# Attention by clusters ahead of two gated layers: products of the identity between TensorE's first steps, centroid norms as steps of the plan, the second pair's loads issued later, and a new table of places

## The chip, the cores and the metric

The kernel runs on one core of one Trainium2 chip. The metric is the device time of one launch in microseconds; the time before is the median of three runs, 766.34 us (765.43 to 766.65). The profile is one execution recorded on the chip. TensorE appears as PE (matmuls) and PEld (weight loads), VectorE as DVE, ScalarE as ACT, GpSimd as POOL, SyncE as SP; SPq and ACTq are the queues from which SyncE and ScalarE issue DMAs.

## What is computed

```python
q_n = q / (norm(q) + 1e-6);  k_n = ...;  c_n = centroids / (norm(centroids) + 1e-6)
q_assign = argmax(einsum('bhsd,hcd->bhsc', q_n, c_n), -1)      # 2 x 8 heads, 768 tokens, D 64, 16 centroids
k_assign = argmax(einsum('bhsd,hcd->bhsc', k_n, c_n), -1)
scores = where(q_assign == k_assign, q @ k.T / 8, -1e9)
attn = exp(scores - max);  attn = attn / (sum(attn) + 1e-9);  x = attn @ v      # (1536, 512)
h = relu(x @ w_in);   x = (h * h) @ w_out                        # d_ff 2048
h = x @ w2_in;        out = (h * cos(h)) @ w2_out
```

## The kernel before

Two heads are worked on together, so there are eight pairs; a pair has 768 queries and 768 keys. For each pair the kernel goes through the same steps, each a small function that issues a few instructions:

- **Preparation.** `load_raw` brings q and k (384 KB each, transposed) into `fq` and `fk`. `sims` multiplies them with the centroid directions `cb` on TensorE (L415); `keep_sims` scales the result by the inverse centroid norms `cn` on ScalarE (L425, tile `sc`); `by_token` transposes it on TensorE (L433); `largest` takes the maximum over the 16 centroids on VectorE (L440, `mx`); `spread` copies it out on ScalarE (L447, `mxb`); `at_max` transposes it back (L456); `compare` (L463), `one_hot` (TensorE, L469) and `keep_one_hot` (VectorE, L476, `ot`) make the one-hot rows of the assignment. `high_part` and `low_part` split q and k into a rounded part and its rest (tiles `set`). `stage`, `stage_oh` and `stage_own` move such rows by DMA into the tiles `ext` (called `xq`, `xk` in the code) and `set`, from which TensorE reads them.
- **Maxima.** `s_max` multiplies one block of queries with half of the keys (L500, four products into a double bank `unit`), `s_largest` takes the row maxima on VectorE (L510); a pair has twelve such steps. After the six of one half, `max_parts` (L519), `max_cast`, `max_rows` (TensorE, L534), `max_keep` and `stage_max` (DMA `set<-mr`) bring the maxima to where the scores need them.
- **Scores.** `scores` (L567, eight products; the last two read the staged maxima), `exponent` on ScalarE (L577), `add_up` on GpSimd (L589, two additions a step), `pv` on TensorE (L597), then `sums` (L612, reads GpSimd's additions) and the steps of the division.

The order of all this is written out: `PLACES` gives each call of each step a number, the steps are sorted by it, and every engine gets its instructions in that order. An engine never overtakes in its own queue. What stands ahead of the sorted steps (L693 to L737) is issued first on each engine: the loads of the first pair, the centroids, their squares, sums, power and inverse (L702 to L704, L734, L735), the zeroing of `ext` on GpSimd (L686), 26 small products of the identity on TensorE (`warm`, L681), and a table for choosing the first of equal maxima (L711 to L726). The second pair's `load_raw` has the places 0 and 11, ahead of nearly everything else, and the first pair's v the place 12.

`small` hands out the one bank (`o_ps[1]`) that all steps of preparation and `sums` share; `unit` hands out one of three double banks. From about 232 us on TensorE works through the two layers (L773, L826), whose order is not in the table.

Of the kernel before, what the change touches and what calls it, by code (L numbers as in the profile page):

```python
# [28 lines left out]
WARM = 26  # L29
N_SPLIT = 54  # L30
# [6 lines left out]
        4, 5, 7, 20, 69, 100, 181, 187, 258, 257, 413, 442, 523, 566, 684, 683,  # L37
    ),
    "low_part": (
        6, 25, 44, 57, 95, 101, 186, 209, 321, 274, 414, 449, 540, 573, 776, 718,  # L40
    ),
# [3 lines left out]
    "sims": (  # L45
        1, 18, 54, 163, 299, 441, 563, 694,
    ),
    "keep_sims": (
        2, 19, 55, 169, 308, 443, 564, 696,
    ),  # L50
    "by_token": (
        3, 28, 67, 216, 349, 477, 610, 726,
    ),
    "largest": (
        8, 29, 68, 217, 350, 479, 612, 728,
    ),
    "spread": (
        9, 30, 77, 230, 356, 497, 624, 737,
    ),
    "at_max": (  # L60
        10, 31, 78, 231, 380, 498, 633, 742,
    ),
    "compare": (
        17, 35, 83, 236, 381, 509, 653, 769,
    ),
    "one_hot": (
        21, 37, 89, 288, 416, 541, 670, 794,
    ),
    "keep_one_hot": (
        23, 41, 140, 293, 423, 552, 671, 810,  # L70
    ),
    "stage_own": (
        32, 93, 282, 327, 332, 652, 611, 751,
    ),
    "stage": (
        16, 14, 60, 42, 200, 160, 277, 279, 415, 405, 587, 570, 719, 677, 799, 798,
    ),
    "stage_oh": (
        24, 72, 159, 307, 433, 589, 698, 839,
    ),  # L80
    "max_parts": (
        58, 80, 143, 184, 244, 302, 403, 447, 504, 593, 635, 713, 788, 848, 883, 962,
    ),
    "max_cast": (
        64, 85, 148, 185, 270, 303, 404, 471, 532, 597, 660, 714, 795, 849, 892, 963,
    ),
    "max_rows": (
        65, 90, 166, 219, 289, 352, 420, 478, 543, 613, 675, 741, 796, 851, 894, 971,
    ),
    "max_keep": (  # L90
        66, 91, 170, 223, 290, 353, 422, 486, 544, 614, 676, 743, 807, 852, 896, 972,
    ),
    "stage_max": (
        73, 127, 171, 238, 304, 354, 431, 488, 558, 636, 691, 762, 811, 871, 929, 984,
    ),
    "cast_selection": (
        13,
    ),
    "constants_own": (
        117, 22, 92,  # L100
    ),
    "constants": (
        48, 63,
    ),
    "move_out": (
        151, 232, 284, 337, 383, 464, 539, 596, 667, 739, 804, 853, 913, 943, 989,
    ),
    "sums": (
        152, 205, 265, 335, 406, 467, 525, 599, 658, 715, 790, 867, 910, 957, 1015,
    ),  # L110
    "move_sums": (
        153, 206, 271, 336, 407, 470, 526, 602, 659, 716, 792, 877, 930, 973, 1016,
    ),
    "deal_sums": (
        182, 218, 305, 338, 417, 502, 583, 603, 672, 738, 800, 891, 933, 992, 1018,
    ),
    "invert": (
        191, 250, 306, 360, 419, 505, 584, 649, 674, 748, 817, 897, 945, 993, 1025,
    ),
    "store_inverse": (  # L120
        240, 269, 339, 361, 455, 524, 590, 650, 717, 754, 845, 907, 949, 994,
    ),
    "load_inverse": (
        259, 276, 340, 372, 456, 536, 631, 682, 732, 775, 846, 908, 966, 995,
    ),
    "divide": (
        260, 325, 398, 399, 483, 537, 645, 704, 733, 834, 861, 934, 999, 1017,
    ),
    "combine_high": (
        261, 363, 418, 424, 550, 595, 697, 711, 744, 835, 880, 935, 1028, 1019,  # L130
    ),
    "combine_low": (
        272, 364, 454, 484, 574, 623, 708, 785, 780, 881, 914, 960, 1029, 1020,
    ),
    "s_max": (
# [5 lines left out]
    ),  # L141
    "s_largest": (
# [5 lines left out]
    ),  # L148
    "scores": (
# [5 lines left out]
    ),  # L155
    "exponent": (
# [35 lines left out]
def tile_kernel(ctx: ExitStack, tc: tile.TileContext, q, k, v, directions, centroids, w1i, w1o, w2i, w2o, out):  # L192
# [137 lines left out]
    def small():  # L330
        return free_small.pop(0)

    def give_small(u):
        free_small.append(u)
# [73 lines left out]

    def sims(n):
        d = pd[n]  # L410
        u = small()
        for i, x in enumerate("qk"):
            for h in range(2):
                g = GC * (2 * i + h)
# [705 lines left out]
```

## Time and profile before

| what | us |
|---|---|
| median of three runs | 766.34 |
| the profiled execution | 766.31 |
| its span | 764.5 |
| TensorE busy | 743.0 (97%) |
| VectorE busy | 584.0 (76%) |
| GpSimd busy | 252.1 (33%) |

The span is what the trace shows from the first to the last instruction; 1.8 us of the profiled execution lie outside it. The busy shares are means over stages with different limits: GpSimd works for most of the first 250 us and hardly afterwards. A line of the timeline gives the start, the duration, the engine, the line of the kernel, the tile written and read, how many instructions were merged, and in brackets the idle time before it with what ended it.

### The profile page before, as it was taken

To read this page: it belongs to the slowest core of one execution; us is meant where nothing else is said; L and a number is where in the kernel's file an instruction comes from. 1 tells how busy PE (TensorE), PEld (TensorE's weight loads), DVE (VectorE), ACT (ScalarE), POOL (GpSimd) and SP (SyncE) were. 2 spreads that over 40 slices of the span, in tenths; PEclk is the share of its full clock that TensorE was granted. 3 is DMA by queue.
4 is the path that set the end of the run, shared out by engine and by line. 5 is a ranking of instruction groups with operands and counts; after the bars stand their busy time and mean duration, and the time that the engine had idled before them with its cause. 6 is when DMAs were issued, how large, how long until landed. Compare 5 with 4: busy or idle time off the path is not lost.

```text
span 764.5 us, 11142 instructions
## 1 busy us (share of the span) xinstructions
PE 743.0 (97%) x4162; PEld 573.7 (75%) x4162; DVE 584.0 (76%) x915; ACT 348.8 (46%) x597; POOL 252.1 (33%) x254
## 2 busy tenths in 40 slices
PE   5899999999999999999999999999999999999998
PEld 2567666667566788888888888888887888888886
DVE  2878879878899999978874119689999766666665
ACT  2256465575464465454445325443434433343332
POOL 6598889999999420000000000012222000000000
PEclk9999999999999999999999999999999999999999
DMA  5531445243345430075300007530000100010001
GB/s 161 173 100 36 132 112 176 79 121 109 118 152 190 153 139 33 29 247 166 111 0 1 1 29 222 190 110 1 0 1 2 55 1 1 0 56 1 0 1 55
DMA packets 43113, 62.35 MB, mean 82 GB/s; under 512 B 8496, under 2 KB 31284, under 8 KB 43060
## 3 DMA queue, kind: packets, MB, share of 16 engines
q1 hardware_dynamic: 42660, 61.03, 25.3%
q10 hardware_dynamic: 400, 0.62, 0.3%
q8 instruction: 32, 0.52, 0.3%
q14 instruction: 21, 0.17, 0.1%
HBM read 48.43 MB, written 5.29 MB: 70 GB/s over the span
## 4 chain that ended last, share of the span: by engine, by line
PE 75%; issue 11%; DMA 5%; POOL 4%; DVE 2%; SPq 1%; ACT 1%; POOLq 0%; ACTq 0%; DVEq 0%
PE bank L826 28%; PE o_ps L773 13%; PE bank L773 13%; PE unit L567 8%; PE o_ps L597 6%; PE unit L500 4%; POOL ewr L811 3%; DMA set<-mr 2%; POOL acc L589 1%; DVE m L510 1%; DMA fk<-in_k_dram 1%; PE o_ps L612 1%; PE o_ps L415 1%; DMA row<-dealt 1%; DMA rb<-row 1%
## 5 line engine op out<-in xcount | busy, mean ns | idle before, releaser
L589 POOL TENSOR_TENSOR acc<-acc,p 128x384 f32<-128x384 f32 x128 | 140.0, 1126 | 0.3 <-ACT p L577 0.3
L826 PE MATMUL bank<-w,ewr 128*128 128x512 f32 x576 | 138.7, 390 | 0.4 <-POOL ewr L811 0.4
L826 PE MATMUL bank<-ewr,w 128*128 128x512 f32 x576 | 138.5, 389 | 0.0
L811 POOL TENSOR_TENSOR ewr<-ews,ewr 128x512 fp32r<-128x512 f32 x24 | 32.4, 1350 | 304.1 <-ACT ewr L807 290.1
L773 PE MATMUL bank<-xh,w 128*128 128x512 f32 x392 | 128.7, 390 | 0.0
L826 PEld LDWEIGHTS bank<-w,ewr 128*128 128x128 f32 x576 | 107.7, 188 | 24.1 <-ACT ewr L807 1.1
L826 PEld LDWEIGHTS bank<-ewr,w 128*128 128x128 f32 x576 | 108.1, 188 | 22.7 <-ACT ews L788 0.3
L773 PE MATMUL o_ps<-xh,w 128*128 128x512 f32 x376 | 123.3, 389 | 0.0
L510 DVE TENSOR_REDUCE m<-unit 128x2 f32<-128x768 f32 x96 | 88.1, 949 | 21.4 <-PE unit L500 18.8
L577 ACT ACTIVATE p<-unit 128x768 f32<-128x768 f32 x96 | 72.2, 815 | 50.5 <-PE unit L567 50.2
L811 DVE TENSOR_TENSOR ewr<-ews,ewr 128x512 fp32r<-128x512 f32 x72 | 49.5, 688 | 55.4 <-ACT ewr L790 50.7
L773 PEld LDWEIGHTS bank<-xh,w 128*128 128x128 f32 x392 | 73.6, 188 | 16.1 <-issue 0.9
L773 PEld LDWEIGHTS o_ps<-xh,w 128*128 128x128 f32 x376 | 70.6, 188 | 14.6
L798 ACT ACTIVATE ews<-ews,narrow_t 128x512 f32<-128x512 f32 x48 | 34.8, 726 | 100.3 <-DVE ews L797 100.3
L773 PE MATMUL bank<-xl,w 128*128 128x512 f32 x196 | 76.3, 389 | 0.0
L773 PE MATMUL o_ps<-xl,w 128*128 128x512 f32 x188 | 73.1, 389 | 0.0
L567 PE MATMUL unit<-set,set 64*128 64x384 f32 x512 | 69.0, 342 | 1.3 <-DMA set<-mr 1.1
L597 PE MATMUL o_ps<-p,rawv 128*64 128x384 f32 x384 | 67.9, 493 | 1.0 <-DMA rawv<-in_v_dram 1.0
L567 PEld LDWEIGHTS unit<-set,set 64*128 64x128 f32 x512 | 48.4, 184 | 9.2 <-DMA set<-mr 3.0
L298 DVE SCALAR_TENSOR_TENSOR top<-wraw,top 128x512 uint32<-128x512 uint32 x64 | 52.1, 815 | 1.6
L296 DVE SCALAR_TENSOR_TENSOR aux<-wraw,aux 128x512 f32<-128x512 uint32 x64 | 52.1, 814 | 1.5
L792 DVE TENSOR_SCALAR ews<-ews 128x512 f32<-128x512 f32 x48 | 20.3, 422 | 42.3 <-ACT ews L802 42.2
(117 smaller groups left out, 1046.1 us busy)
## 6 DMA issues: line engine op xcount, KB each, us to landing
wraw<-in_moe_w_in_dram SPq DMA_DIRECT2D x32, 512.0 KB, 4.5
wraw<-in_moe_w_out_dram SPq DMA_DIRECT2D x32, 512.0 KB, 3.5
rawv<-in_v_dram SPq DMA_DIRECT2D x8, 384.0 KB, 5.3
ext<-set SPq DMA_DIRECT2D x32, 96.0 KB, 2.3
rb<-row SPq DMA_DIRECT2D x32, 96.0 KB, 2.7
fq<-in_q_dram SPq DMA_DIRECT2D x7, 384.0 KB, 5.1
fk<-in_k_dram SPq DMA_DIRECT2D x7, 384.0 KB
held<-kept SPq DMA_DIRECT2D x8, 256.0 KB, 3.2
```

The source lines that it names most:

```text
L296: cost(690, lambda: ve.scalar_tensor_tensor(restf, low, 2.0**-32, rest, ALU.mult, ALU.add)),
L298: cost(690, lambda: ve.scalar_tensor_tensor(top, high, 0xC0000000, top, ALU.bitwise_and, ALU.bitwise_or)),
L500: nc.tensor.matmul(u[:, j, :HALF], lhsT=a[r, qs], rhs=b[r, ks], start=(p == 0), stop=(p == 1))
L510: nc.vector.tensor_reduce(d["m"][:, i, :, kh], u[:, :, :HALF], AX, ALU.max)
L567: nc.tensor.matmul(u[:, j, :HALF], lhsT=a[r], rhs=b[r, qs], start=(p == 0), stop=(p == len(ops) - 1))
L577: nc.scalar.activation(t, u[:, :, :HALF], AF.Exp, scale=SCALE)
L589: nc.gpsimd.tensor_tensor(accs[hb][:, j], a[:, j], ptiles[u_][:, j], ALU.add)
L597: nc.tensor.matmul(o_ps[0][j * D : (j + 1) * D, :HALF], lhsT=raw[n, "v"][:, kt, j, :], rhs=t[:, j], start=(kt == 0), stop=(kt == NT - 1),)
L773: nc.tensor.matmul(ph, lhsT=w[:, a, :], rhs=x[blk][:, a, :], start=(a == i == 0), stop=(a == KD - 1 and i == 2))
L798: nc.scalar.activation(e2, e2, AF.Sin, bias=hpi)
L811: e.tensor_tensor(al, e2, ah.bitcast(F32), ALU.subtract)
L826: nc.tensor.matmul(y, lhsT=a, rhs=b, start=(idx in opens and i == 0), stop=(idx in closes and i == 2))
```

## The change

`keep_warm`, a product of the identity with three copies of itself (384 columns, into `o_ps[0]`), is added and called 38 times, at places from 4 to 108. The centroid norms become steps: `squares`, `norms` and `inverses`, once for the first pair's column and once for the other three, with the centroids loaded in two pieces (32 KB by ScalarE's queue, 96 KB by SyncE's). The zeroing of `ext` for the first pair goes from GpSimd to VectorE and the first pair's rounded q from VectorE to ScalarE. The second pair's preparation takes its bank from `unit` in place of `small`. All other steps are the same instructions at other places.

```diff
 PLACES = {
...
     "load_raw": (
-        12, 0, 11, 129, 27, 26, 278, 45, 94, 370, 110, 128, 568, 392, 344, 727, 472, 556, 847, 555, 664, 915,
+        112, 13, 37, 177, 74, 82, 385, 176, 165, 402, 335, 280, 496, 436, 288, 771, 555, 618, 886, 590, 557,
+        935,
     ),
...
-    def small():
-        return free_small.pop(0)
+    def small(n=0):
+        return unit() if n == 1 else free_small.pop(0)
...
+    def keep_warm():
+        nc.tensor.matmul(
+            o_ps[0][:, :HALF].rearrange("p (a c) -> p a c", c=P), lhsT=identr,
+            rhs=identr.unsqueeze(1).to_broadcast([P, HT, P]), start=True, stop=True,
+        )
...
-    nc.scalar.dma_start(cw, centroids)
+    nc.scalar.dma_start(cw[:, :1], centroids[:, :1])
     load_raw(0, "k", (nc.sync, nc.scalar))
+    nc.sync.dma_start(cw[:, 1:], centroids[:, 1:])
     nc.scalar.activation(eps, half_t, AF.Exp)
-    constants(nc.gpsimd, xq[0])
-    nc.vector.tensor_tensor(cw, cw, cw, ALU.mult)
-    nc.vector.tensor_reduce(cn, cw, AX, ALU.add)
-    nc.gpsimd.tensor_tensor(cn, cn, half_t.to_broadcast([P, NP]), ALU.pow)
     nc.gpsimd.memset(eps, 1e-9)
+    which = slice(0, 1), slice(1, NP)
+
+    def squares(i):
+        w = which[i]
+        nc.vector.tensor_tensor(cw[:, w], cw[:, w], cw[:, w], ALU.mult)
+        nc.vector.tensor_reduce(cn[:, w], cw[:, w], AX, ALU.add)
+
+    def norms(i):
+        w = which[i]
+        nc.gpsimd.tensor_tensor(cn[:, w], cn[:, w], half_t.to_broadcast([P, w.stop - w.start]), ALU.pow)
+
+    def inverses(i):
+        w = which[i]
+        nc.vector.tensor_scalar(cn[:, w], cn[:, w], 1e-6, None, ALU.add)
+        nc.vector.reciprocal(cn[:, w], cn[:, w])
...
     warm(WARM)
-    nc.vector.tensor_scalar(cn, cn, 1e-6, None, ALU.add)
-    nc.vector.reciprocal(cn, cn)
-    constants(nc.gpsimd, xk[0])
+    constants(nc.vector, xq[0])
+    constants(nc.vector, xk[0])
...
-            at(high_part, n, x, *(() if n else (nc.vector,)))
+            at(high_part, n, x, *((nc.vector,) if n == 0 and x == "k" else ()))
...
+    for i in range(2):
+        for f in (squares, norms, inverses):
+            at(f, i)
     at(cast_selection)
+    for i in range(N_WARM):
+        at(keep_warm)
```

The lines of the changed kernel stand 15 to 37 lower than before: sims L430, by_token L448, at_max L471, one_hot L484, s_max L515, scores L582, `keep_warm` L699.

On TensorE the first pair's preparation is followed, before, by the second pair's, in the one bank `o_ps_66` (these are the rows behind the 26 small products):

```order
L415 MATMUL o_ps_66<-fq_123,cb 32x384 x2
L415 MATMUL o_ps_66<-fk_128,cb 32x384 x2
L433 MATMUL o_ps_66<-ident,sc_192 128x128 x3
L456 MATMUL o_ps_66<-ident,mxb_203 128x128 x3
L415 MATMUL o_ps_66<-fq_186,cb 32x384 x2
L415 MATMUL o_ps_66<-fk_208,cb 32x384 x2
L469 LDWEIGHTS first_of
L469 MATMUL o_ps_66<-eq_220,first_of 128x384
L433 MATMUL o_ps_66<-ident,sc_226 128x128 x3
L456 MATMUL o_ps_66<-ident,mxb_252 128x128 x3
L500 MATMUL unit_70<-set_1_106,set_0_105 128x384 x2
```

The same place now (`fq_123` and `fk_128` are the first pair, `fq_208` and `fk_241` the second):

```order
L699 MATMUL o_ps_65<-identr 128x384 x2
L430 MATMUL o_ps_66<-fq_123,cb 32x384 x2
L430 MATMUL o_ps_66<-fk_128,cb 32x384 x2
L699 MATMUL o_ps_65<-identr 128x384 x10
L448 MATMUL o_ps_66<-ident,sc_210 128x128 x3
L699 MATMUL o_ps_65<-identr 128x384 x7
L471 MATMUL o_ps_66<-ident,mxb_229 128x128 x3
L699 MATMUL o_ps_65<-identr 128x384 x3
L484 LDWEIGHTS first_of
L484 MATMUL o_ps_66<-eq_243,first_of 128x384
L699 MATMUL o_ps_65<-identr 128x384 x5
L430 MATMUL unit_70<-fq_208,cb 32x384 x2
```

Ten, seven, three and five products stand ahead of the four steps that follow, and the second pair's similarities come behind the first pair's one-hot; its at_max comes five s_max later than before.

On SyncE's queue, before, the second pair's loads (`fq_186`, `fk_208`) and v stand right behind the first pair's k:

```order
L380 DMA fq_123<-in_q_dram 64x768
L697 DMA cb<-in_directions_dram 128x128
L380 DMA fk_128<-in_k_dram 64x768
L380 DMA fq_186<-in_q_dram 128x768
L380 DMA fk_208<-in_k_dram 128x768
L375 DMA rawv_210<-in_v_dram 128x768
L405 DMA ext_1_118<-set_1_106 32x768 x2
L270 DMA wraw_0_0_216<-in_moe_w_in_dram 128x4x256
```

The same place now (`ext_1_118` is staged from the rounded k of the first pair, `set_1_106`):

```order
L395 DMA fq_123<-in_q_dram 64x768
L718 DMA cb<-in_directions_dram 128x128
L395 DMA fk_128<-in_k_dram 64x768
L721 DMA cw<-in_centroids_dram 128x192
L285 DMA wraw_0_0_200<-in_moe_w_in_dram 128x4x256
L420 DMA ext_1_118<-set_1_106 32x768 x2
L395 DMA fq_208<-in_q_dram 128x768
L395 DMA fk_241<-in_k_dram 128x768
```

A weight block of 512 KB is now what is issued right behind the first pair's k; the second pair's loads stand behind the staging of `set_1_106`, and v has gone further back.

On VectorE, now, the first rows are these (the centroids' first column is `128x64`, `narrow_t` holds the norms, `set_1_106` is the first pair's rounded k):

```order
L707 MEMSET ext_0_117 32x768 x2
L707 MEMSET ext_1_118 32x768 x2
L728 TENSOR_TENSOR cw<-cw 128x64
L729 TENSOR_REDUCE narrow_t<-cw 128x1
L712 MEMSET set_0_113 32x256 x2
L712 MEMSET set_1_114 32x256 x2
L712 MEMSET set_2_115 32x256 x2
L404 CAST set_1_106<-fk_128 128x768
L737 TENSOR_SCALAR narrow_t<-narrow_t 128x1
L738 RECIPROCAL narrow_t<-narrow_t 128x1
L455 TENSOR_REDUCE mx_225<-o_ps_66 128x24
```

Before, the inverse norms stood ahead of both roundings of the first pair, and no memset stood here.

## Rows read from the trace of the kernel before

**Rows 1.** Busy time of each engine in three stretches.

```profile
0.00:33.00 33.00, 20.84 (x123) 11.09 (x123) 16.59 (x27) 7.87 (x15) 21.85 (x45) 1.00 0.54 161
33.00:250.00 217.00, 211.92 (x1795) 141.68 (x1797) 184.81 (x229) 122.80 (x218) 198.21 (x186) 1.00 0.42 125
250.00:760.00 510.00, 509.61 (x2246) 420.75 (x2247) 381.46 (x659) 217.75 (x364) 32.02 (x25) 1.00 0.17 57
```

**Rows 2.** Whom TensorE waited for from 0 to 33 us: total, times, longest.

```profile
PE o_ps L415 <- DMA fk<-in_k_dram: 2.7, 1, 2.7
```

**Rows 3.** Whom TensorE waited for from 33 to 250 us.

```profile
PE o_ps L612 <- POOL acc L589: 1.7, 2, 0.9
```

**Rows 4.** Timeline of TensorE: the small products, first and later steps.

```profile
1.71 2.95 PE L681 MATMUL o_ps<-identb 128*128 128x128 bf16 x26 [1.71 <-DVE identb L226]
9.21 1.50 PE L415 MATMUL o_ps<-fk,cb 128*32 128x384 f32 x4 [2.65 <-DMA fk<-in_k_dram]
11.47 0.87 PE L433 MATMUL o_ps<-ident,sc 128*128 128x128 f32 x3 [0.77 <-ACT sc L425]
...
22.89 0.52 PE L500 MATMUL unit<-ext,ext 64*128 64x384 f32 x2
...
24.81 0.35 PE L500 MATMUL unit<-set,set 64*128 64x384 f32 x2
...
30.54 0.52 PE L433 MATMUL o_ps<-ident,sc 128*128 128x128 f32 x3
...
32.91 0.62 PE L567 MATMUL unit<-set,set 64*128 64x384 f32 x4
```

**Rows 5.** Timeline of VectorE: squares, rounding of k, first reduction, maxima.

```profile
7.02 0.43 DVE L702 TENSOR_TENSOR cw<-cw 128x256 f32<-128x256 f32 x1 [5.24 <-DMA cw<-in_centroids_dram]
...
10.30 1.17 DVE L389 CAST set<-fk 128x768 fp32r<-128x768 f32 x1
...
22.84 1.82 DVE L510 TENSOR_REDUCE m<-unit 128x2 f32<-128x768 f32 x2 [0.34 <-PE unit L500]
...
29.49 0.15 DVE L519 TENSOR_REDUCE m<-m 128x6 f32<-128x12 f32 x1
```

**Rows 6.** Timeline of ScalarE, of SyncE's queue and of GpSimd.

```profile
10.75 0.58 ACT L425 ACTIVATE sc<-o_ps,narrow_t 128x384 f32<-128x384 f32 x1 [6.35 <-PE o_ps L415]
...
11.50 1.22 SPq L405 DMA_DIRECT2D ext<-set  x2
...
38.88 1.98 POOL L589 TENSOR_TENSOR acc<-p,p 128x384 f32<-128x384 f32 x2
```

**Rows 7.** Stretches as in rows 1; the last number is GB/s moved.

```profile
0.00:5.00 5.00, 2.95 (x26) 2.69 (x26) 0.36 (x2) 1.49 (x2) 2.45 (x12) 1.00 0.59 158
5.00:10.00 5.00, 2.29 (x8) 0.40 (x8) 1.69 (x5) 0.00 (x0) 1.85 (x3) 1.00 0.80 268
```

**Rows 8.** The chain that ended last: start us, us, what.

```profile
2.33 6.83 DMA fk<-in_k_dram
```

**Rows 9.** DMA issues of the page: KB each, median us to landing.

```profile
ext<-set SPq DMA_DIRECT2D x32, 96.0 KB, 2.3
...
fq<-in_q_dram SPq DMA_DIRECT2D x7, 384.0 KB, 5.1
```

**Rows 10.** Groups on VectorE and ScalarE from 0 to 24 us, busy, mean ns.

```profile
L440 DVE TENSOR_REDUCE mx<-o_ps 128x24 f32<-128x384 f32 x2 | 1.1, 557 | 2.0 <-PE o_ps L433 2.0
L447 ACT COPY mxb<-mx 128x384 f32<-128x384 f32 x2 | 1.0, 511 | 3.2 <-DVE mx L440 3.2
L463 DVE TENSOR_TENSOR eq<-sc,o_ps 128x384 bf16<-128x384 f32 x2 | 1.1, 554 | 3.1 <-PE o_ps L456 3.1
L476 DVE TENSOR_SCALAR ot<-o_ps,oh_above,oh_scale 128x384 fp32r<-128x384 f32 x1 | 0.7, 677 | 2.9 <-PE o_ps L469 2.9
```

**Rows 11.** Groups of GpSimd and VectorE from 33 to 250 us.

```profile
L589 POOL TENSOR_TENSOR acc<-acc,p 128x384 f32<-128x384 f32 x128 | 140.0, 1126 | 0.3 <-ACT p L577 0.3
...
L691 DVE MEMSET set<- 32x256 f32 x6 | 1.6, 272 | 0.4
```

More of the change, by code (lines that the diff above doesn't have):

```diff
@@ L29 @@
 WARM = 26
+N_WARM = 38
 N_SPLIT = 54
@@ L44 @@
+        935,
     ),
     "sims": (
-        1, 18, 54, 163, 299, 441, 563, 694,
+        6, 52, 98, 215, 359, 469, 632, 730,
     ),
     "keep_sims": (
-        2, 19, 55, 169, 308, 443, 564, 696,
+        14, 58, 99, 217, 368, 472, 643, 731,
     ),
     "by_token": (
-        3, 28, 67, 216, 349, 477, 610, 726,
+        25, 63, 109, 265, 397, 529, 651, 772,
     ),
     "largest": (
-        8, 29, 68, 217, 350, 479, 612, 728,
+        26, 64, 114, 281, 398, 538, 656, 777,
     ),
     "spread": (
-        9, 30, 77, 230, 356, 497, 624, 737,
+        28, 72, 120, 282, 414, 551, 657, 779,
@@ L59 @@
     ),
     "at_max": (
-        10, 31, 78, 231, 380, 498, 633, 742,
+        36, 91, 121, 287, 415, 552, 665, 787,
     ),
     "compare": (
-        17, 35, 83, 236, 381, 509, 653, 769,
+        38, 97, 122, 291, 422, 564, 673, 788,
     ),
     "one_hot": (
-        21, 37, 89, 288, 416, 541, 670, 794,
+        42, 111, 147, 330, 458, 587, 703, 831,
     ),
     "keep_one_hot": (
-        23, 41, 140, 293, 423, 552, 671, 810,
+        45, 117, 148, 341, 460, 588, 717, 836,
     ),
     "stage_own": (
-        32, 93, 282, 327, 332, 652, 611, 751,
+        75, 170, 235, 283, 515, 568, 821, 944,
@@ L74 @@
     ),
     "stage": (
-        16, 14, 60, 42, 200, 160, 277, 279, 415, 405, 587, 570, 719, 677, 799, 798,
+        46, 10, 125, 104, 242, 220, 369, 353, 452, 446, 589, 576, 757, 687, 856, 863,
     ),
     "stage_oh": (
-        24, 72, 159, 307, 433, 589, 698, 839,
+        53, 143, 207, 362, 461, 601, 759, 864,
     ),
     "max_parts": (
-        58, 80, 143, 184, 244, 302, 403, 447, 504, 593, 635, 713, 788, 848, 883, 962,
+        95, 138, 196, 257, 318, 381, 439, 502, 580, 611, 688, 762, 817, 888, 949, 999,
@@ L92 @@
     ),
     "stage_max": (
-        73, 127, 171, 238, 304, 354, 431, 488, 558, 636, 691, 762, 811, 871, 929, 984,
+        123, 164, 231, 275, 354, 424, 468, 521, 594, 637, 708, 780, 851, 909, 981, 1030,
+    ),
+    "squares": (
+        0, 27,
+    ),
+    "norms": (
+        2, 56,
+    ),
+    "inverses": (
+        12, 57,
     ),
     "cast_selection": (
-        13,
+        7,
+    ),
+    "keep_warm": (
+        4, 5, 15, 16, 17, 18, 19, 20, 21, 22, 23, 24, 29, 30, 31, 32, 33, 34, 35, 39, 40, 41, 47, 48, 49, 50,
+        51, 59, 60, 61, 62, 76, 77, 85, 86, 90, 92, 108,
@@ L98 @@
     ),
     "constants_own": (
-        117, 22, 92,
+        1, 69, 81,
     ),
     "constants": (
-        48, 63,
+        100, 101,
     ),
     "move_out": (
-        151, 232, 284, 337, 383, 464, 539, 596, 667, 739, 804, 853, 913, 943, 989,
+        213, 232, 336, 358, 466, 546, 593, 666, 727, 805, 877, 921, 969, 1012, 1049,
     ),
     "sums": (
-        152, 205, 265, 335, 406, 467, 525, 599, 658, 715, 790, 867, 910, 957, 1015,
+        200, 254, 320, 386, 453, 517, 572, 645, 693, 764, 824, 885, 938, 1010, 1062,
@@ L119 @@
     ),
     "store_inverse": (
-        240, 269, 339, 361, 455, 524, 590, 650, 717, 754, 845, 907, 949, 994,
+        266, 311, 361, 435, 544, 603, 672, 719, 758, 807, 873, 942, 997, 1042,
     ),
     "load_inverse": (
-        259, 276, 340, 372, 456, 536, 631, 682, 732, 775, 846, 908, 966, 995,
+        312, 374, 445, 444, 563, 629, 677, 736, 786, 822, 893, 952, 1026, 1050,
     ),
     "divide": (
-        260, 325, 398, 399, 483, 537, 645, 704, 733, 834, 861, 934, 999, 1017,
+        342, 396, 470, 478, 583, 682, 713, 752, 815, 846, 933, 1000, 1054, 1055,
@@ L328, in tile_kernel, with give_small @@
     free_small = [o_ps[1].rearrange("p (a c) -> p a c", a=1)]
[L330 to L334 removed]
+    def small(n=0):
+        return unit() if n == 1 else free_small.pop(0)
+    def give_small(u, n=0):
+        (free_units if n == 1 else free_small).append(u)
     def unit():
@@ L410, in sims @@
         d = pd[n]
-        u = small()
+        u = small(n)
         for i, x in enumerate("qk"):
@@ L425, in keep_sims @@
         nc.scalar.activation(sc, u[:, 0, :HALF], AF.Copy, scale=cn[:, pairs[n][1] : pairs[n][1] + 1])
-        give_small(u)
+        give_small(u, n)
     def by_token(n):
         d = pd[n]
-        u = small()
+        u = small(n)
         for t in range(HT):
@@ L440, in largest @@
         nc.vector.tensor_reduce(mx, u[:, 0, :HALF].rearrange("p (g c) -> p g c", c=NC), AX, ALU.max)
-        give_small(u)
+        give_small(u, n)
     def spread(n):
@@ L452, in at_max @@
         d = pd[n]
-        u = small()
+        u = small(n)
         for t in range(HT):
@@ L463, in compare @@
         nc.vector.tensor_tensor(eq, d["sc"], u[:, 0, :HALF], ALU.is_equal)
-        give_small(u)
+        give_small(u, n)
     def one_hot(n):
         d = pd[n]
-        u = small()
+        u = small(n)
         nc.tensor.matmul(u[:, 0, :HALF], lhsT=first_of, rhs=d["eq"], start=True, stop=True)
```

24 lines of the change are left out of this document (12 added, 12 removed), and 66 rows, old and new, of the table PLACES.

## The prediction

> **What bounds the kernel now.** I read the busy time by stretches first. The reader is to see that TensorE works for 211.9 of the 217 us from 33 to 250 us, and for 509.6 of 510 us after that, but only for 20.8 of the first 33 us [rows 1]. So the end moves with the moment at which TensorE becomes full, less whatever work was done before that moment, and the change's edits all lie ahead of it. GpSimd is close behind: 198.2 of 217 us. Then I read whom TensorE waits for. Before 33 us the longest single wait is for the first pair's k, 2.7 us [rows 2]; from 33 to 250 us all its idle time is 217 - 211.9 = 5.1 us, of which 1.7 us are waits of the sums for GpSimd's additions [rows 3]. The timeline shows a second loss in the first stretch: the same three transposes take 0.87 us at 11.47 and 0.52 us at 30.54, and a pair of 384-column products takes 0.52 us at 22.89 and 0.35 us at 24.81 [rows 4]. Until about 24 us TensorE therefore works at its slower pace, although the column of the granted clock says 1.00 throughout [rows 1]; it has stood idle for 12.2 of the first 33 us. It gets faster only after a stretch without gaps. Last I followed the order of the first pair: k lands at 2.33 + 6.83 = 9.16 us [rows 8], similarities to 10.71, scaled ones at 10.75 [rows 4, 6], first reduction at 22.84, the seventh done and the first maxima taken at 29.49 [rows 5], first scores at 32.91 [rows 4].
>
> **Loads.** Until k lands, the core has moved 5 x 158 + 4.16 x 268 = 1905 KB [rows 7], of the 2112 KB that were issued (four loads of 384 KB and v, plus 64 and 128 KB). k's own place in the queues is at 960 KB, so it shared the engines with what stood behind it. Now q, k, directions and both centroid pieces are 960 KB and the weight block behind them 512 KB: 1472 KB. At the same rates 790 KB are there at 5 us and the rest 682/268 = 2.5 us later: k lands at 7.5 if it must share with all of it, and at 5.6 if with nothing. I take 7.5, since the row of before shows nearly full sharing.
>
> **Norms and k's rounding.** The centroids landed at 7.02 [rows 5], behind half of q; 32 KB in place of 128 KB can't come before q is there (about 5) nor later than 7; I take 6. VectorE then runs two small steps (0.15 each, as the reduction of twelve columns at 29.49), six memsets of 0.272 [rows 11], done at 7.9. Then it rounds k, 1.17 [rows 5], to 9.1, and only behind that come the two steps of the inverse, to 9.4. The scaled similarities need 0.58 [rows 6] and are there at 10.0 (11.33 before). The four memsets of `ext` on VectorE are hidden by the wait for the centroids: four of 768 columns are at most 4 x 3 x 0.272 = 3.3 us from 1.8, and if this cover were gone they would cost 3.3 us there.
>
> **Products of the identity.** The trace has none of 384 columns. The small product of 128 took 2.95/26 = 0.113 us [rows 4], 1.13 columns a ns, the lower of the clock's two levels (1.2 GHz); three times that is 0.34, and 0.17 at the upper one (2.4 GHz). The ten ahead of by_token start behind k's similarities. If these still run slowly (1.50, [rows 4]), they end at 9.0, the ten at 12.4, and by_token would be 2.4 us behind its data. If TensorE has become fast by then (26 small ones, two large ones and q's similarities from 1.7 to about 7 nearly without a gap), the ten end at 7.5 + 0.75 + 1.7 = 10.0, just as the data come. The Trainium skill ("TensorE: Matmul & The Clock Gate", section "What's actually happening") says that the throttled clock is the default state and that activity releases it; the change of pace in the trace at about 24 us, after the gapless run of the first s_max, agrees, while the profile's granted-clock column doesn't show it. By that rule alone the ten would run at the fast pace and cost nothing. I take a change of pace in the midst of the ten: by_token at 11.2. The later seven, three, five and four (1.2, 0.5, 0.9, 0.7 us) lie beside `largest` and `spread`, `compare`, the load of the second pair and its scaling, all at least as long. The last seven lie where TensorE waits for VectorE's 0.91 us per reduction; uncovered they would cost 7 x 0.17 = 1.2 us.
>
> **The one-hot's path.** From by_token: 0.52 + 0.56 + 0.51 + 0.52 + 0.55 + 0.3 (the one product of one_hot, an estimate from the 384-column price) + 0.68 [rows 4, 10], with seven hand-overs of about 0.1: 4.3 us, so 15.5; issue of the second half 0.6 and landing 2.3 [rows 6, 9]: 18.4.
>
> **The second pair's path.** Its loads now stand behind the staging of rounded k: 9.1 + 1.2 for two issues [rows 6] = 10.3, landing after 5.1 [rows 9] for q, 15.4, and k at 15.2 to 15.9; lower bound 768/268 + 2.3. I take 15.5. Similarities of k 0.8, scaling 0.58, transposes 0.52: 17.4. Only then does TensorE's queue reach the first s_max; its `ext` products want the one-hot at 17.6 and get it at 18.4. I count half of this 0.8 us, as the pace is open: 0.4.
>
> **Sum.** From 17.4: `largest` of the second pair 0.56, six reductions of 0.91 [rows 5], maxima 0.15: 23.6, against 29.49. Then on VectorE, ahead of the first scores in TensorE's queue: `compare` 0.55, two reductions 1.8, `largest` of the third pair 0.56; on ScalarE `spread` 0.51, on TensorE at_max 0.52, and three hand-overs: 27.8, against 32.91 [rows 4]. That is 5.1 us earlier. Two s_max that came before the first scores now come behind: 2 x 2 x 0.17 = 0.7 us of work not yet done. 5.1 - 0.7 - 0.4 = 4.0 us. GpSimd's first addition needs the fourth exponent, about four scores later, 32 against 38.88 [rows 6], so it is no bound. For the rest of the table, whose steps are all moved, I put nothing: the same work, TensorE full. Bounds: its 5.1 us of idle time could go entirely, or double. The profiled execution is 766.31 us, the runs' median 766.34, so no correction: **762.3 us**.
>
> **Rivals.** *Slow pace throughout the first pair.* by_token at 12.4, one-hot there at about 21 (each step of TensorE twice as long, seven products 2.4 us ahead of at_max): s_max starts 3.4 us later than in my sum, a gain of 1, 765.3 at worst, some 764.3 if the pace changes at the second group. For: 26 small products did not change it before. Against: the queue is much fuller now. *Absorbed later.* The stretch to 250 us gives the 4 us back, in waits for staged maxima or for GpSimd: 766.3. For: GpSimd is busy for 91% there. Against: it starts 6 us earlier too. *Slower: sums ahead of their additions.* In the table the first sums now come two places behind their last addition (198, 200), before 13 (139, 152). If the new order expects GpSimd one step (2 x 1.126 us, [rows 11]) too early at five of the fifteen sums, TensorE stands for 11 us: 762.3 + 11 = 773; it decides from a mean wait of 4/15 = 0.27 us above today's 1.7/15. For: 91% busy. Against: by my count the tenth addition of the first sums ends at 43 us, when TensorE gets there too. *More.* The order also takes away most of the 5.1 us: 758.5.
>
> **Numbers.** My sum with 2.5 to 6 us gained: 0.60. More than that: 0.11. Slow pace: 0.12, half of it within the bound. Absorbed: 0.10. Slower: 0.07. A difference under 0.2% (1.5 us) can't be told from no change. Faster 0.60 + 0.11 + 0.06 = 0.77, same 0.06 + 0.10 = 0.16, slower 0.07. The likeliest case alone spans 760.3 to 763.8; the range, 758.8 to 765.5, takes in most of the case of more and the slow pace, and leaves out the loss and most of the absorbed gain.
>
> **What would show it.** k's similarities at about 7.5; scaled ones at 9.4; by_token at 0.52 us, not 0.87; first reduction at 18 to 19; first scores at 27 to 29; 4 us less idle time before 33 us and about 5 us from there to the layers. Wrong if by_token starts later than its data by over 2 us, if the second pair's k lands after 17, or if sums wait over 6 us in total.

## The result: 758.25 us, and the profile after

The changed kernel takes 758.25 us (median of four runs, 758.09 to 758.74), the kernel before beside it 766.5 (four runs, 765.43 to 770.15); the ratio is 0.9885, with a 95% interval of 0.9852 to 0.9918. Its profiled execution took 758.1 us with a span of 756.1. The sign was right; the gain is 8.2 us where 4.0 were forecast, and the time lies 0.5 us below the range.

The timeline of the changed kernel, in the order in which [rows 4 to 6] show the steps of before (start us, duration us, engine, line, what; the new line numbers):

```profile
7.22 0.88 PE L430 MATMUL o_ps<-fk,cb 128*32 128x384 f32 x4 [0.39 <-DMA fk<-in_k_dram]
8.03 2.01 PE L699 MATMUL o_ps<-identr 128*128 128x384 f32 x10
9.88 0.49 PE L448 MATMUL o_ps<-ident,sc 128*128 128x128 f32 x3
17.15 0.44 PE L515 MATMUL unit<-set,set 64*128 64x384 f32 x2
27.41 0.61 PE L582 MATMUL unit<-set,set 64*128 64x384 f32 x4
7.98 0.56 DVE L404 CAST set<-fk 128x768 fp32r<-128x768 f32 x1
8.64 0.16 DVE L738 RECIPROCAL narrow_t<-narrow_t 128x1 f32<-128x1 f32 x1
17.84 1.82 DVE L525 TENSOR_REDUCE m<-unit 128x2 f32<-128x768 f32 x2
8.90 0.58 ACT L440 ACTIVATE sc<-o_ps,narrow_t 128x384 f32<-128x384 f32 x1 [1.74 <-DVE narrow_t L738]
31.96 1.97 POOL L604 TENSOR_TENSOR acc<-p,p 128x384 f32<-128x384 f32 x2 [0.27 <-ACT p L592]
```

The first scores start at 27.41 us, 5.5 earlier than before, and two of the `s_max` that came ahead of them are still to do (0.7 us). So 4.8 us come from the start. The rest shows when both spans are cut at the first scores and behind the last sums, where only the two layers are left (length of the stretch, busy time of PE, PEld, DVE, ACT, POOL with the number of instructions, then granted clock, DMA share, GB/s), the kernel before first:

```profile
0.00:32.91 32.91, 20.75 (x122) 11.00 (x123) 16.50 (x27) 7.87 (x15) 21.76 (x45) 1.00 0.54 161
32.91:250.40 217.49, 212.41 (x1798) 141.87 (x1797) 185.27 (x230) 123.17 (x219) 198.69 (x186) 1.00 0.42 125
```

```profile
0.00:27.41 27.41, 23.92 (x151) 15.26 (x151) 20.71 (x40) 9.77 (x17) 17.31 (x41) 1.00 0.59 167
27.41:242.00 214.59, 211.58 (x1806) 141.91 (x1805) 183.24 (x224) 124.96 (x220) 203.89 (x187) 1.00 0.45 130
242.00:751.60 509.60, 509.19 (x2246) 420.42 (x2243) 381.01 (x658) 216.43 (x362) 31.83 (x25) 1.00 0.17 57
```

From the first scores to that point it was 217.49 us and is 214.59, although 0.7 us more work lies in it: 3.6 us saved there, and 4.8 + 3.6 is the 8.4 by which the spans differ. Of the 3.6, TensorE's idle time gives 5.08 - 3.01 = 2.1. The other 1.5 were hidden in what the column calls busy: it fell by 0.8 while the work grew by 0.7. Within unbroken runs of scores, one score started more than 0.85 us behind the last seven times before and once now (0.70 is the usual), which is 4.3 us over the usual in all, against 0.8; a part of this is in the idle time above. What TensorE's matmuls waited for in that stretch, before (beside [rows 3]) and after:

```profile
PE unit L567 <- DMA set<-mr: 1.9, 5, 0.8
```

```profile
PE o_ps L627 <- POOL acc L604: 1.5, 3, 0.6
PE unit L549 <- ACT set L540: 0.8, 1, 0.8
PE unit L582 <- DMA set<-mr: 0.6, 1, 0.6
```

Waits for GpSimd are what they were; the waits for staged maxima are a third, but in a second record of the kernel before (before_again, below) they are 0.4 us, so one record doesn't settle this.

### The profile page after: what moved, and what is told of

Read it like the earlier page. It is cut to its first block, busy times and chain, and to the rows that moved or that the text cites. A ratio compares the mean times of both kernels' runs of the same rounds, so it can differ in the third digit from the quotient of the medians.

```text
span 756.1 us, 11197 instructions
## 1 busy us (share of the span) xinstructions
PE 745.4 (99%) x4200; PEld 577.9 (76%) x4200; DVE 586.1 (78%) x922; ACT 351.6 (46%) x598; POOL 253.0 (33%) x251
## 4 chain that ended last, share of the span: by engine, by line
PE 77%; issue 11%; POOL 8%; DVE 1%; DMA 1%; ACT 1%; POOLq 0%; ACTq 0%; DVEq 0%
PE bank L858 28%; PE o_ps L805 13%; PE bank L805 13%; PE unit L582 7%; PE o_ps L612 7%; PE unit L515 5%; POOL acc L604 4%; POOL ewr L843 3%; PE o_ps L627 1%; POOL xl L691 1%; PE o_ps L430 1%; DMA set<-mr 1%; DVE m L525 1%; DMA fk<-in_k_dram 1%; PE o_ps L699 1%
## 5 line engine op out<-in xcount | busy, mean ns | idle before, releaser
L604 POOL TENSOR_TENSOR acc<-acc,p 128x384 f32<-128x384 f32 x128 | 142.5, 1146 | 2.3 <-ACT p L592 2.3
L805 PEld LDWEIGHTS o_ps<-xh,w 128*128 128x128 f32 x376 | 70.5, 188 | 14.6
L582 PE MATMUL unit<-set,set 64*128 64x384 f32 x512 | 66.5, 340 | 0.0
L306 DVE SCALAR_TENSOR_TENSOR w<-aux,aux 128x512 fp32r<-128x512 f32 x64 | 51.1, 799 | 1.7
```

Of the source, the lines that this page charges most:

```text
L306: ve.scalar_tensor_tensor(w[:, 1], restf, 2.0**-20, power.bitcast(F32), ALU.mult, ALU.mult)
L582: nc.tensor.matmul(u[:, j, :HALF], lhsT=a[r], rhs=b[r, qs], start=(p == 0), stop=(p == len(ops) - 1))
L604: nc.gpsimd.tensor_tensor(accs[hb][:, j], a[:, j], ptiles[u_][:, j], ALU.add)
L805: nc.tensor.matmul(ph, lhsT=w[:, a, :], rhs=x[blk][:, a, :], start=(a == i == 0), stop=(a == KD - 1 and i == 2))
```

## Experiments: what each part is worth

Below, "the stretch" runs from the first scores to the end of the last sums, some 514 us ahead of the end of the span in both kernels; a few products of the layers lie in it too, from 231.6 us before and from 223.8 now. Every run has runs of the kernel before on the same chip beside it, and ratios are to those, with a 95% interval in brackets.

**old_order_products**: the order before with the 38 products laid into it.

```diff
+    "keep_warm": (0.5, 0.5, 2.5, ..., 53.5, 61.5),
```

(with the function `keep_warm` and its 38 calls)

> The kernel before with the 38 products of the identity put between the same steps as in the changed kernel, nothing else changed. Theory (the pace of the first 24 us is worth 2 to 3 us, but k's landing at 9.2 and the ten products behind k's similarities stand against it): 763.5 to 765.5 us, transposes at 0.5 us from the second group on. Rival (26 small products did not change the pace and k's wait of 2.7 us lets it fall again): 766.4 to 768.

Measured 761.99 us, 0.9964 (0.9940 to 0.9987), below either forecast. by_token takes 0.49 us at 10.12, and the first scores start at 29.60. The recorded execution is one of the faster (760.41 us), and its stretch, in the old order, is 0.4 us longer than that of the kernel after, with 0.7 us less work in it:

```profile
29.60:244.57 214.97, 211.43 (x1798) 141.73 (x1797) 185.62 (x230) 122.85 (x219) 201.20 (x186) 1.00 0.42 126
```

**old_head_new_tail**: the places of before up to the first scores, the new ones from there.

```diff
-    places from 81 on: those of before
+    places from 81 on: those of after, from its 124 on
```

> The kernel before up to its first scores, then all steps that are left in the order of the changed kernel. Theory (the order of the long stretch brings about 3.6 us by itself): 766.4 - 3.6 = 762.8 us, TensorE's idle time behind the first scores 3 us instead of 5. Rival (the long stretch is shorter only because GpSimd and the loads are ahead after the earlier start): 766.4 +- 0.7.

762.2 us, 0.9960 (0.9942 to 0.9977): the new order of the long stretch is worth some 3 us by itself (1.8 to 4.4), though no edit of the diff but its table acts there.

**old_head_products_new_tail**: both together.

> The old order up to the first scores with the 38 products laid into it, the new order from there; loads and norms as before. Theory (products and new tail each bring their own 3 to 4 us in the old head): 758.5 to 760.5, ratio about 0.992. Rival (what the products brought in the old order, 3.5 us, was mostly the same waits of the tail that the new tail order removes): 761.5 to 762.5, ratio about 0.995, no better than either alone.

760.9 us, 0.9932 (0.9906 to 0.9958), between the two forecasts. In ratios the two add up as far as intervals of 0.2 to 0.3% can show it (0.36% and 0.40%, together 0.68%), which leaves 0.3 to 0.5% to the loads, the norms and the new preparation (the kernel after stands at 0.9885 and, in a second series, 0.9903).

**new_head_old_tail**: the other way round, after up to its place 124 and then before.

> The changed kernel up to its first scores, then all steps that are left in the order of the kernel before. Theory (start 5.5 us earlier with 0.7 us of work left over, the long stretch as before): 766.4 - 4.8 = 761.6 us. Rival (the earlier start shortens the long stretch too, by GpSimd's lead): 758.3 to 759.3.

764.64 us, 0.9990 (0.9970 to 1.0009). Both theories missed. The first scores start at 29.49, just behind the joint TensorE stands 1.6 us for `ext<-ot`, and the stretch takes 217.8 us. By the median nearly all of the earlier start is given back when the rest is not laid out for it. The recorded execution (763.09 us, of 761.99 to 767.79) doesn't show this: its span is 3.1 us shorter than that of before. Where the median loses it stays open.

**no_products**: the kernel after without `keep_warm`.

```diff
-N_WARM = 38
+N_WARM = 0
```

> The changed kernel without its 38 products of the identity; every other step at its place. Theory (the products bring the fast pace early and lie beside waits): TensorE stays at the slow pace until the first s_max, the transposes of the first pair take 0.87 us and not 0.5, first scores 2 to 3 us later than 27.4, time 760.2 to 761.5 us. Rival (the loads, the norms and the order alone bring what was gained): 758.3 +- 0.4.

758.88 us, 0.9918 (0.9896 to 0.9941), against 0.9885 and 0.9903 (0.9873 to 0.9932) for the kernel after: nothing that these runs can tell apart, and its profile ends 0.9 us later. The theory was right on the transposes (0.87 us) and wrong on what they cost: the first scores come at 28.15, 0.7 us later. In the new order the products are worth little, in the old one 0.36%, some 2.8 us (1.0 to 4.6).

**early_loads**: the kernel after with the second pair's loads behind the first k, as before.

```diff
-        112, 13, 37, 177, ...
+        112, -1, -0.5, 177, ...
```

> The kernel after with the second pair's two loads issued right behind the first pair's k, as before, all else as after. Theory (k shares the DMA engines with what stands behind it, so the early loads cost it time): k's similarities start at 8.5 to 9.2 in place of 7.2, the first scores 1.2 to 2 us later, 759.5 to 760.2. Rival (with a weight block of 512 KB behind k in either order the sharing is nearly the same, and the second pair comes earlier, which gives something back): k at 7.2 to 7.8 and 758.0 to 758.6.

759.2 us, 0.9907 (0.9882 to 0.9932), between the two forecasts; k's similarities at 7.32. The theory was wrong: in the recorded execution k is not later with the second pair behind it than with a weight block there. Whether k shares with either of them isn't tested, since something is queued behind it in both.

## Experiments: where the long stretch gained

**before_again**: the kernel before, recorded once more.

> The kernel before, unchanged, recorded once more: how much of its profile belongs to the order and how much to the one execution. Theory (the order makes the waits): the first pair's k lands at 9.2 us again, the first scores start at 32.9, and the stretch from there to the layers takes 217.5 us with about 1.9 us of waits for staged maxima and 1.0 for v. Rival (the moment at which the first loads land varies from run to run, and the rest follows it): k lands anywhere from 7.5 to 9.2, the first scores move with it by up to 1.7 us, and the waits for staged maxima come out differently, so that the stretch takes 215 to 218.

766.27 us, span 764.4. k's similarities start at 7.64, not 9.21, from the same queue, yet the first scores only at 34.33, since TensorE keeps its lower pace to 35 us; the stretch takes 215.97. So start and stretch share the 764.4 differently each time. With the 214.0 of after_again (below), the 214.97 of old_order_products and the 0.7 us of work, the stretch's gain is anything from 1 to 4 us, by the pair of records that is compared. One thing is the same in all profiles of the old order: maxima that are ready stand in SyncE's queue. The kernel before, the half whose maxima are ready at 90.70 (ScalarE, then SyncE's queue, then TensorE):

```profile
90.24 0.46 ACT L541 CAST mr<-unit 64x384 fp32r<-64x384 f32 x1
...
90.88 0.43 SPq L638 DMA_DIRECT2D row<-dealt  x1
92.64 1.14 SPq L644 DMA_DIRECT2D rb<-row  x2
93.83 0.58 SPq L380 DMA_DIRECT2D fk<-in_k_dram  x1
94.50 0.57 SPq L548 DMA_DIRECT2D set<-mr  x1
...
97.73 0.82 PE L567 MATMUL unit<-set 64*128 64x384 f32 x2 [0.75 <-DMA set<-mr]
```

`rb<-row` waits for the inverse that `row<-dealt` has just sent off, and the maxima stand behind it for 3.8 us. Over all 16 halves they stand some 16 and 15 us in the two profiles of before, and under 2 in the kernel after, where other DMAs lie between the two of an inverse more often (10 of 15 inverses, 6 of 16 before). The kernel after:

```profile
84.81 0.47 ACT L556 CAST mr<-unit 64x384 fp32r<-64x384 f32 x1
...
85.30 1.18 SPq L563 DMA_DIRECT2D set<-mr  x2
```

The standing by itself need not cost anything. In old_order_products the maxima stand for 14.6 us too, and TensorE's matmuls wait for them only 0.2 us; it costs where the scores get there first.

**maxima_first**: the order before, six of these maxima moved forward on SyncE's queue.

```diff
-    load_inverse: 276, 340, 631, 682     store_inverse: 754
+    load_inverse: 304.3, 354.3, 636.3, 691.3     store_inverse: 762.3
```

(and three other DMAs alike)

> The order before, with nothing moved on TensorE, VectorE, ScalarE or GpSimd: on SyncE's queue alone six staged maxima (of the halves 2, 4, 5, 9, 10 and 11) go ahead of DMAs that stood before them (four loads of inverses, a store of one, three others). In two profiles of the kernel before, 7 of its 16 pairs of maxima, ready in mr, stand for 1.1 to 3.8 us behind such DMAs, 14.8 us in all; in the changed kernel one does, for 1.4. Theory (this queue is what the new order saves in the long stretch): the standing falls below 5 us, TensorE's weight loads wait under 1 us for staged maxima in place of 4.2 and 1.9, the stretch takes about 215 us and the time falls by 1.5 to 3 us, 763.0 to 764.7. Rival (what is saved there comes back as waits for banks and GpSimd): 765.4 to 766.8.

765.92 us, 1.0012 (0.9991 to 1.0034); the standing fell to some 7 us, not below 5, and the stretch is 217.6. The theory fell. At the same place the scores now stand for VectorE (TensorE, then VectorE):

```profile
98.53 0.69 PE L541 MATMUL unit<-set,set 64*128 64x384 f32 x2 [2.33 <-DVE m L484]
```

```profile
95.10 0.90 DVE L270 SCALAR_TENSOR_TENSOR aux<-wraw,aux 128x512 f32<-128x512 uint32 x1
95.93 1.21 DVE L271 TENSOR_SCALAR top<-wraw 128x512 uint32<-128x512 uint32 x1
97.06 0.54 DVE L437 TENSOR_TENSOR eq<-sc,o_ps 128x384 bf16<-128x384 f32 x1
97.53 0.94 DVE L484 TENSOR_REDUCE m<-unit 128x2 f32<-128x768 f32 x1
```

The reduction that frees the scores' bank is queued behind two steps that split a weight block and a compare. In before it ended at 99.28, and the scores that need it started at 99.34, while the maxima had let the earlier ones go on at 97.73: the reduction ends last there, with or without the maxima.

**maxima_and_reductions_first**: as the last, the two splitting steps behind that reduction.

```diff
-    split_one: 373, 374
+    split_one: 385.2, 385.4
```

> The order before with the six staged maxima moved forward on SyncE's queue as in the run maxima_first, and on VectorE two steps that split a weight block moved behind the reduction of the last s_max ahead of the scores at 95 us. Theory (in the old order the maxima and this reduction ended together, so only both moves bring what the new order brought): no wait of over 1 us for VectorE or for staged maxima in the long stretch, which takes 214.5 to 215.5 us in place of 217.6, and 762 to 764 us. Rival (the old order meets a third wait at the same place, and the new order's gain can't be had by such moves): a stretch of 216.5 to 218 us and 765 to 766.8 us.

767.38 us, 1.0030 (1.0002 to 1.0058), a stretch of 219.1. This theory fell too; the longest wait now comes some five us further on, up to 104.71:

```profile
PE o_ps L443 <- ACT r L593: 2.6, 1, 2.6
```

**late_maxima**: the other direction, the kernel after with six of its staged maxima set back to the first scores' places.

```diff
-    stage_max: 354, 468, 594, 637, 708, 780
+    stage_max: 369.5, 494.5, 611.5, 661.5, 720.5, 791.5
```

> The kernel after with six staged maxima (of the halves 4, 6, 8, 9, 10 and 11) set back on SyncE's queue, behind the DMAs that now follow them, to just ahead of the place of the first scores that read them; nothing else moved. Theory (scores reach maxima that are not there, and a full TensorE never makes that up): six stalls of 0.4 to 1.5 us, 761 to 765, and the weight loads' waits for staged maxima up from about 1 to over 4 us. Rival (the scores have enough other work ahead, or the waits for GpSimd shrink by as much): 758.0 to 758.8.

763.61 us (762.07 to 767.11), 0.9978 (0.9959 to 0.9996): 5 us lost, as the theory had it. The recorded execution is the slowest of the twelve (767.11 us), and 2.8 us of its loss lie ahead of the first scores (next section); its stretch takes 220.7 us in place of 214.6. TensorE's weight loads wait 5.4 us for maxima, its matmuls 3.1, and a long wait costs more than itself. Timeline and stretches of late_maxima behind its longest one (the seventh number of a stretch is the granted clock):

```profile
83.97 0.44 PE L554 MATMUL unit<-set,set 64*128 64x384 f32 x1 [2.04 <-DMA set<-mr]
86.03 0.83 PE L554 MATMUL unit<-set 64*128 64x384 f32 x2
```

```profile
85.80:88.00 2.20, 2.20 (x18) 2.20 (x18) 0.00 (x0) 1.66 (x3) 0.00 (x0) 0.53 0.62 203
88.00:92.00 4.00, 4.00 (x37) 2.93 (x35) 3.11 (x4) 2.86 (x6) 2.93 (x4) 0.83 0.01 1
92.00:96.00 4.00, 4.00 (x33) 2.27 (x31) 3.37 (x6) 2.86 (x7) 3.58 (x5) 1.00 0.61 136
```

Two products take 0.83 us there and 0.34 elsewhere: behind the stall the record shows the lower of the two clocks (1.2 GHz) for about 3 us, from 85.9 to 89.3.

So it is shown by the times that the new table gains behind the first scores (old_head_new_tail), and that setting maxima back loses it. That moving six of them forward is enough is refuted, and so is one pair of waits behind one another. Which set of moves would do it in the old order stays open.

One rival is untested. GpSimd is nearly as full as TensorE (203.9 of the 214.6 us in the kernel after), and the last sums wait for its last additions in either kernel (before, then after):

```profile
249.96 0.52 PE L612 MATMUL o_ps<-acc,ones 128*32 128x192 f32 x4 [0.75 <-POOL acc L589]
241.68 0.52 PE L627 MATMUL o_ps<-acc,ones 128*32 128x192 f32 x4 [0.62 <-POOL acc L604]
```

From GpSimd's first addition to the end of its last it took 211.0 us before and takes 209.7 now, and 208.5 to 211.2 in every profile but that of late_maxima (215.7), whatever the order. No run shortens its work, so how far GpSimd bounds what an order can gain stays open.

## Experiments: TensorE's pace at the start

**no_late_products**: the kernel after without its last seven products.

```diff
-    keep_warm: ..., 62, 76, 77, 85, 86, 90, 92, 108
+    keep_warm: ..., 62
```

> The kernel after without its last seven products, those between the first s_max, where TensorE waits for VectorE's reductions; the first 31 stay. Theory (TensorE falls back to the lower pace when it stands between the s_max, as it did for 7 us when it stood 1.6 us there in the kernel with the tighter head): s_max, at_max or by_token at the lower pace somewhere from 18 to 27 us, first scores 0.5 to 3 us later, 759 to 761. Rival (gaps of 0.2 to 0.4 us change no pace, the seven fill time that VectorE sets): pace and first scores unchanged, 758.0 to 758.6.

757.87 us, 0.9907 (0.9886 to 0.9928): as the rival had it, they are worth nothing that shows.

**tighter_head**: from the kernel after, VectorE's squares, inverses and six memsets out of the first pair's way, and 34 products.

```diff
-    squares: 0, 27   norms: 2, 56   inverses: 12, 57   constants_own: 1   high_part: .., 43   keep_warm: ten ahead of by_token
+    squares: 0, 45.2   norms: 2, 45.5   inverses: 12, 45.8   constants_own: 57.5   high_part: .., 53.2   keep_warm: four
```

> The kernel after with small steps of VectorE moved out of the first pair's way (six memsets of set and the squares of the later centroid columns behind the first one-hot, the inverses ahead of the splitting of a weight block), ScalarE's rounding of the second q behind the issue of the one-hot, and 34 products in place of 38, four in place of ten ahead of by_token. Theory (the end follows the first s_max, and this follows VectorE's steps ahead of compare and the one-hot): k's rounding 0.7 us and compare 1.3 us earlier, first s_max at about 15.8 in place of 17.15, first scores about 1.3 us earlier, 756.7 to 757.3. Rival (the second pair's k, or the pace with fewer products, takes the place of what is removed): first s_max after 16.8, or products at half the pace, 758.0 to 759.0.

760.98 us, 0.9925 (0.9898 to 0.9951). by_token starts at 8.68 and the first s_max at 16.04, 1.1 us earlier, nearly as planned. But `largest` of the second pair stood behind the memsets, TensorE stood 1.6 us for it, the record shows the lower clock from 19.4 to 26.2, and the first scores came at 30.52:

```profile
16.50 0.34 PE L487 MATMUL unit<-set,set 64*128 64x384 f32 x2
18.63 0.44 PE L487 MATMUL unit<-set,set 64*128 64x384 f32 x2 [1.62 <-DVE mx L427]
21.82 0.69 PE L487 MATMUL unit<-set,set 64*128 64x384 f32 x2
```

```profile
19.90:26.40 6.50, 6.50 (x28) 3.37 (x27) 4.07 (x6) 1.52 (x2) 6.15 (x10) 0.51 0.33 94
```

**tighter_head_2**: the memsets on GpSimd, 38 products; run twice, the second time beside **after_again**, the kernel after unchanged.

```diff
-    at(constants_own, nc.vector, 2)
+    at(constants_own, nc.gpsimd, 2)      # at 69.5
```

> The kernel with the tighter head once more, its six memsets on GpSimd ahead of its second subtraction, where they delay nothing of VectorE's, and 38 products again (five ahead of by_token, nine ahead of the second pair's similarities, five behind them). Theory (the tighter head failed only by the 1.6 us for which TensorE stood behind the memsets, and the pace that this cost): no stall over 0.6 us and no lower pace, first reduction at about 16.7 in place of 17.84, first scores 1.0 to 1.3 us earlier, 757.0 to 757.5. Rival (the scores' start is held by something else, or the end by GpSimd): first scores earlier by less than 0.5 us or the time unchanged, 758.0 to 758.8.

> The kernel after, unchanged, on one chip with the next kernel. Theory (its start is safe, since the products and VectorE's early steps leave TensorE no long gap): all times within 757.8 to 759, k's similarities and by_token at the faster pace. Rival (it only mostly is: where k lands late, the ten products run at the lower pace and the first scores come about 3 us later, as in the profile of the kernel with late maxima): single times of 760 to 762 among the others.

> The second kernel with the tighter head, unchanged, beside the kernel after on the same chip. Theory (first scores 1.1 us earlier, and the end follows): median 1.0 us below that of the kernel after. Rival (the lead is lost in the long stretch, which took 215.2 us against 214.6): within 0.3 us of it.

First 757.18 us, 0.9895 (0.9876 to 0.9915), first scores at 26.33; then 759.12 (757.69 to 759.66) against 758.32 (757.89 to 759.42) for the kernel after, so neither forecast of the second run came. In the second profile k's similarities start at 8.15, behind 1.77 us of standing, and the five products behind them take 1.74 us, the lower pace. The changed kernel's start can do the same, though none of its six times here goes above 759.42; in late_maxima, whose steps of the first 15 us are the changed kernel's, k's similarities came at 8.16 behind 1.33 us of standing:

```profile
8.16 1.50 PE L402 MATMUL o_ps<-fk,cb 128*32 128x384 f32 x4 [1.33 <-DMA fk<-in_k_dram]
9.59 3.57 PE L671 MATMUL o_ps<-identr 128*128 128x384 f32 x10
12.95 0.84 PE L420 MATMUL o_ps<-ident,sc 128*128 128x128 f32 x3
```

Its first scores started at 30.24, 2.8 us later than in the kernel after. **bridged** and **tighter_bridged** fill that standing, in the kernel after and in tighter_head_2:

```diff
         for i, x in enumerate("qk"):
+            for _ in range(5 if n == 0 and i else 0):
+                keep_warm()
```

> The kernel after with five more products of the identity between the similarities of the first q and those of the first k, where TensorE stands for k's load (0.4 us in one profile, 1.0 and 1.3 in others). Theory (the standing ahead of k is what throws TensorE back to the lower pace): products at 0.2 us and by_token at about 0.5 in every run, times within 757.8 to 758.8, none above. Rival (it delays k's similarities by up to 1 us where k is early, and the pace has other reasons): 758.5 to 759.5, with single times above.

> The second kernel with the tighter head with the same five products between q and k. Theory: the faster pace throughout, first reduction at 16.7 to 17.2, median 757.0 to 757.5, 0.8 to 1.2 us below the kernel bridged on the same chip. Rival (VectorE and the second pair's loads set the start of the maxima however TensorE runs, or k's late landing does): 758 to 759, no better than the kernel bridged.

bridged takes 758.53 us (758.18 to 758.70), tighter_bridged 757.80 (756.97 to 758.18), four runs each on one chip; ratios to before 0.9912 (0.9897 to 0.9926) and 0.9900 (0.9884 to 0.9917). In neither profile does the pace fall back, and k's similarities start some 0.8 us later than in the kernel after. The start of bridged:

```profile
5.33 1.50 PE L404 MATMUL o_ps<-fq,cb 128*32 128x384 f32 x4
6.75 1.34 PE L673 MATMUL o_ps<-identr 128*128 128x384 f32 x5
8.09 0.84 PE L404 MATMUL o_ps<-fk,cb 128*32 128x384 f32 x4
8.85 2.01 PE L673 MATMUL o_ps<-identr 128*128 128x384 f32 x10
```

tighter_bridged lies between its two forecasts, 0.7 us below bridged and about 0.5 below the changed kernel, no more than its runs scatter (1.2 us).

## Why the prediction was wrong

**The step that failed** is "For the rest of the table, whose steps are all moved, I put nothing: the same work, TensorE full." What was put at nothing came out at 3.6 us in the profile, and the order of the stretch alone gave 0.40%, some 3 us, in old_head_new_tail. TensorE was not full. 5.1 us of idle time were read from [rows 1], and as their lower bound the prediction let them all go, but kept that for a case of 0.11; and 211.9 us of busy time were taken for work, while some 1.5 us of it were short waits inside runs of scores that merged matmuls hide. Of the 5.1, [rows 3] was given only the waits for GpSimd, which stayed; 1.9 us for maxima and 1.0 for v were not looked at. The prediction's own sign, about 5 us of idle time left there, came out at 3.0. Which waits the new order removes, beyond those for maxima in this pair of records, stays open.

**The start**, 4.8 us for 4.0, was sound step by step. k's similarities at 7.22 (7.5 forecast), the inverse done at 8.80 (9.4), scaling from 8.90 (9.4), first reduction at 17.84 (18.0), first scores at 27.41 (27.8), GpSimd's first addition at 31.96 (32). Of the 0.8 us, 0.4 are the earlier scores, and 0.4 the wait for the one-hot, which the sum charged and which didn't come: the first `ext` products followed at 17.43 without a gap.

**Loads.** The time was right and its reason not shown: the sharing read from k's 9.21 was largely that one execution's, since 7.64, 8.5 and 7.48 came from the same queue order, and early_loads left k where it was. With the new queue k's similarities started anywhere from 7.0 to 8.2, so that 7.22 met 7.5 so well is in part luck.

**Products.** "A change of pace in the midst of the ten" was not seen: they ran at 0.20 us each from the start, by_token came at 9.88 instead of 11.2, and in another execution all ten ran at 0.36, which is the rival of the slow pace, at 2.8 us. What they are worth in the old order, some 2.8 us, the forecast didn't price apart, and most of it is not needed in the new one. The clock column of 1.00, against which the prediction read the slower pace, was no reading ahead of 24.2 us (last section).

**Norms.** Rounding k took 0.56 us, not the 1.17 of [rows 5]; that row lay beside GpSimd's zeroing (below). The 0.6 us are the inverse's 8.8 against 9.4.

**Rivals.** *Sums ahead of their additions* did not come: 1.5 us of waits in three, as [rows 3]. *Absorbed later* failed too, but the median of new_head_old_tail shows it for an order that doesn't fit its start. *More* has the number, 758.25 for 758.5, but that is partly luck: it wanted most of the 5.1 us of idle time, and 2.1 of them went; 1.5 us of hidden waits and 0.8 of the start made up the rest.

## What to carry to other kernels

A table that moves every step is itself an edit with a price, and the first bound on its gain is the whole idle time of the stretch that it orders, plus what merged rows hide; here about half of that came. Look in each DMA queue for ready data that stand behind an issue which waits; but a wait taken away is a gain only where nothing else ends beside it, so look for the second one first. A stall of two us on TensorE can cost itself and a few us at half pace behind it: 3 us behind 2.0 in late_maxima, 7 us behind 1.6 in tighter_head, though none behind 1.6 in new_head_old_tail.

## What the runs showed of the hardware

Two steps of VectorE take longer beside GpSimd. Squaring 192 columns took 1.50 us in the kernel after, while GpSimd subtracted from 10.41 to 12.24, and 0.35 us in tighter_head_2, where GpSimd was idle:

```profile
10.95 1.50 DVE L728 TENSOR_TENSOR cw<-cw 128x192 f32<-128x192 f32 x1
```

```profile
12.64 0.35 DVE L700 TENSOR_TENSOR cw<-cw 128x192 f32<-128x192 f32 x1
```

In all seven profiles in which the two lie beside one another the squares took 1.1 to 1.7 us and ended 0.2 us behind the subtraction; in the five others they took 0.35. The Trainium skill ("SBUF — State Buffer", section "Who interferes with whom") says that an operation of VectorE with two inputs from SBUF contends with one of GpSimd that reads SBUF, by an exclusive lock. By that rule the squares wait until 12.24 and end soon after; they ended at 12.45.

Rounding k took 1.17 us from 10.30 in before, where GpSimd zeroed `ext` until 11.05, and 0.56 us in the kernel after, where GpSimd was idle. That GpSimd is the reason isn't shown here: all profiles of the old start have the zeroing beside it and none of the new ones has.

A stretch's granted clock is printed as 1.00 where the record has no entry yet. by_token took 0.87 us at 9.58, half pace, in no_products and in before_again; the first lies in a stretch printed with 1.00, and in the second the stretch behind it has 0.50:

```profile
5.00:20.00 15.00, 10.57 (x40) 4.35 (x42) 9.86 (x24) 5.13 (x10) 8.20 (x18) 1.00 0.66 191
```

```profile
10.00:35.00 25.00, 19.52 (x91) 10.89 (x91) 15.36 (x21) 5.41 (x12) 17.41 (x30) 0.50 0.45 133
```

The trace of no_products has its first entry of the clock at 21.1 us, the full level; that of before has it at 24.2, where the pace changes in [rows 4]; before_again has the full level from 4.6 and half from 8.0. So ahead of the first entry the column says nothing, and the duration of a known shape is the sign to go by.
